# Attention kernel: scores and maxima move into one shared PSUM tile, with one order of steps per head and 17 exponentials of twice the width

## The chip, the cores and the metric

The kernel runs on one core of one Trainium2 chip. The metric is the time of one execution on the device in microseconds (us). Three runs of the kernel before took 2745.0 to 2745.48 us, with a median of 2745.36 us.

## What is computed

Two attention blocks, A and B, read the same `x` of 2048 rows and 512 columns and are mixed by a gate for each row:

```python
def _A_ref(x, wqkv, wo):          # _B_ref is the same with B's weights
    H = 32; Dh = D // H           # 32 heads of 16
    qkv = (x @ wqkv).reshape(B, S, 3, H, Dh).transpose(2, 0, 3, 1, 4)
    q, k, v = qkv[0], qkv[1], qkv[2]
    scores = jnp.einsum("bhqd,bhkd->bhqk", q, k) * (Dh ** -0.5)
    p = _softmax(scores, axis=-1)
    o = jnp.einsum("bhqk,bhkd->bhqd", p, v)
    return o.transpose(0, 2, 1, 3).reshape(B, S, D) @ wo

x = A_x
g = _sigmoid((x * gate_w).sum(-1, keepdims=True))
return g * _A_ref(x, A_wqkv, A_wo) + (1 - g) * _B_ref(x, B_wqkv, B_wo)
```

Two blocks of 32 heads make 64 heads, each with 2048 x 2048 scores of depth 16.

## The kernel before, in words

A first stage projects q, k and v for both blocks and writes them to device memory. Then comes the long stage that the change touches. It counts in rounds, 16 to a head and 1024 in all. A round is 128 keys of one head: four score matmuls (L210), each of 128 keys by 512 queries into one PSUM bank, four exponentials on ScalarE (L212, 512 columns each) that write the tile `p`, and products of `p` with v that TensorE adds up in the bank `acc` (L689). After a head's last round ScalarE copies `acc` out (L710). The row maxima that softmax needs are computed 22 rounds (`NT + LEAD`) ahead, for a later head. For two tiles of 128 queries there are six plain maxima (`max_plain`, a matmul at L148 and a `tensor_reduce` on VectorE at L153) and one pair: `max_rise` puts the positive part of a difference through ScalarE (L160), and `max_pair` lets VectorE add it to a bank of scores and take the maximum (L165).

All matmuls of scores and maxima have 48 or 50 rows, and `rows` (L129) gives them alternately the lower and the upper half of the array, so that two neighbours in TensorE's queue run side by side. The products use the whole array.

PSUM has eight banks of 512 fp32 columns. Before, three of them are the pool `ps_m` (maxima), four the pool `ps_st` (scores and rises), and one is `acc`. Each pool hands out its banks in turn. Each engine works through its own queue in order. What a matmul waits for is the read that last used its bank.

The order of the long stage is written out as strings, one letter for a step: `e` a score and its exponential, `m` a plain maximum, `D` a rise, `A` a pair, and a digit n for n products of a quarter round each (four matmuls of 17 columns and 128 queries for a quarter; neighbouring quarters of one round are joined). `FULL` (L724) covers four rounds, and `EDGE` (L725) replaces halves of it around a head's start and end:

```python
FULL = "mme3emmeem4meeemAe", "3emmeeem3meeemA3DeD"
EDGE = "eemm4mDmemDe3emeemAe", "3emmeeem3emem3eAe"
```

The loop at L744 runs these strings. Where the digit stands, it also starts the projections of finished heads (`project_out`), and one row operation that is due (`row_ops`: gates, reciprocals and a head's `max_split` and `max_rows`). The last 22 rounds, with no maxima left, run `LATE`.

## Time and profile before

| what | value |
|---|---|
| median of 3 runs | 2745.36 us (2745.0 to 2745.48) |
| span of the profiled execution | 2743.5 us; the page has no other time for it |
| granted TensorE clock over the span | 1.000 |
| PE busy | 2733.8 us (100%), 25446 instructions |
| DVE busy | 2411.5 us (88%), 4473 instructions |
| ACT busy | 2410.8 us (88%), 4794 instructions |
| from the first to the last copy of `acc` on ScalarE (62 copies) | 325.0 to 2659.8 us |

A span is the time from the first to the last instruction of one execution as the hardware profiler saw it. Busy time counts an instruction from its start to its end, so an engine whose instructions overlap is counted once. Matmul ends are modelled, and a busy PE can still be waiting. PE is TensorE's matmuls, PEld its weight loads, DVE is VectorE, ACT is ScalarE. "Idle before, released by" in the views names the event that came last before an instruction started.

### The profile page before, as it was taken

To read this page: it belongs to the slowest core of one execution; us is meant where nothing else is said; L and a number is where in the kernel's file an instruction comes from. 1 tells how busy PE (TensorE), PEld (TensorE's weight loads), DVE (VectorE), ACT (ScalarE), POOL (GpSimd) and SP (SyncE) were. 2 spreads that over 40 slices of the span, in tenths; PEclk is the share of its full clock that TensorE was granted. 3 is DMA by queue.
4 is the path that set the end of the run, shared out by engine and by line. 5 is a ranking of instruction groups with operands and counts; after the bars stand their busy time and mean duration, and the time that the engine had idled before them with its cause. 6 is when DMAs were issued, how large, how long until landed. Compare 5 with 4: busy or idle time off the path is not lost.

```text
span 2743.5 us, 64283 instructions
## 1 busy us (share of the span) xinstructions
PE 2733.8 (100%) x25446; PEld 1418.7 (52%) x25446; DVE 2411.5 (88%) x4473; ACT 2410.8 (88%) x4794; POOL 262.2 (10%) x467
## 2 busy tenths in 40 slices
PE   9999999999999999999999999999999999999998
PEld 7787544444444444444444555544444444445543
DVE  5444899999999999999999978899999999998895
ACT  4222899999999999999999978899999999998787
POOL 2010112110000000000100232000000001002202
PEclk9999999999999999999999999999999999999999
DMA  8583434333333233333423534223333333344312
GB/s 286 181 262 153 93 74 81 62 70 62 74 67 60 52 60 67 62 64 62 85 52 54 123 78 92 48 49 62 78 62 63 59 66 65 62 87 83 80 36 95
DMA packets 95603, 231.25 MB, mean 84 GB/s; under 512 B 26182, under 2 KB 35878, under 8 KB 82758
## 3 DMA queue, kind: packets, MB, share of 16 engines
q1 hardware_dynamic: 91590, 216.65, 36.1%
q0 software_dynamic: 2560, 8.91, 1.1%
q8 instruction: 201, 3.29, 0.6%
q10 hardware_dynamic: 1152, 1.57, 0.2%
q14 instruction: 100, 0.82, 0.1%
HBM read 158.13 MB, written 68.94 MB: 83 GB/s over the span
## 4 chain that ended last, share of the span: by engine, by line
PE 99%; DVE 1%; DMA 0%; issue 0%; SPq 0%; DVEq 0%; POOL 0%; POOLq 0%
PE acc L689 38%; PE ps_st L210 24%; PE ps_m L148 19%; PE ps_st L290 6%; PE ps_st L148 5%; PE ps_st L343 3%; PE ps_m L558 3%; PE ps_st L558 0%; PE ps_m L84 0%; PE ps_st L299 0%; DVE o_acc L575 0%; DMA o_num<-od 0%; DVE mxp L153 0%; PE ps_m L210 0%; DVE rise L165 0%; DMA od<-ev 0%
## 5 line engine op out<-in xcount | busy, mean ns | idle before, releaser
L212 ACT ACTIVATE p<-ps_st 128x512 f32<-128x512 f32 x4050 | 2076.8, 629 | 95.3 <-PE ps_m L148 56.1
L153 DVE TENSOR_REDUCE mxp<-ps_m 128x1 f32<-128x512 f32 x3048 | 1934.8, 684 | 125.2 <-PE ps_st L148 46.0
L210 PE MATMUL ps_st<-q_st,k_st 50*128 50x512 f32 x4054 | 1269.5, 433 | 0.0
L148 PE MATMUL ps_m<-k_st,q_st 48*128 48x512 f32 x3548 | 1223.8, 439 | 0.3
L689 PE MATMUL acc<-p,vg 128*17 128x128 f32 (+3 forms) x15664 | 1129.8, 392 | 0.5 <-DVE ev L703 0.4
L210 PEld LDWEIGHTS ps_st<-q_st,k_st 50*128 50x128 f32 x4054 | 614.0, 184 | 436.4 <-ACT p L212 382.7
L148 PEld LDWEIGHTS ps_m<-k_st,q_st 48*128 48x128 f32 x3548 | 604.2, 184 | 268.7 <-DVE mxp L153 222.1
L689 PEld LDWEIGHTS acc<-p,vg 128*17 128x17 f32 x15664 | 323.1, 96 | 404.2 <-issue 330.7
L165 DVE CUSTOM_DVE_ANT_0 rise<-ps_m,rise 128x512 f32<-128x512 f32 x500 | 341.2, 682 | 16.6 <-PE ps_m L148 13.1
L160 ACT ACTIVATE rise<-ps_st 128x512 f32<-128x512 f32 x500 | 300.1, 601 | 16.6 <-PE ps_st L210 0.8
L148 PE MATMUL ps_st<-x_st,q_st 48*128 48x512 f32 x500 | 195.4, 451 | 0.0
L175 POOL CAST mparts<-mrow 128x16 fp32r<-128x16 f32 x64 | 12.7, 198 | 1875.9 <-DVE mrow L174 1875.9
L148 PEld LDWEIGHTS ps_st<-x_st,q_st 48*128 48x128 f32 x500 | 78.0, 184 | 119.5 <-ACT p L212 119.2
L310 ACT CAST part<-ps_st 128x512 fp32r<-128x512 f32 x64 | 37.0, 589 | 111.6 <-PE ps_st L290 95.6
L311 DVE TENSOR_TENSOR part<-ps_st,part 128x512 fp32r<-128x512 f32 x64 | 43.7, 690 | 93.7 <-ACT part L310 70.2
L346 ACT COPY v_st<-ps_st 128x512 f32<-128x512 f32 x32 | 18.8, 588 | 84.2 <-PE ps_st L343 82.5
L558 PE MATMUL ps_m<-wo,ot 128*128 128x512 f32 x348 | 83.0, 393 | 1.0
L558 PEld LDWEIGHTS ps_m<-wo,ot 128*128 128x128 f32 x348 | 64.4, 188 | 19.6 <-issue 4.6
L290 PE MATMUL ps_st<-xh,whi 128*128 128x512 f32 x224 | 59.9, 389 | 0.0
L290 PE MATMUL ps_st<-xh,wlo 128*128 128x512 f32 x224 | 59.9, 389 | 0.0
L290 PE MATMUL ps_st<-xl,whi 128*128 128x512 f32 x224 | 59.9, 389 | 0.0
L545 POOL TENSOR_TENSOR o_num<-o_num,rb 128x512 f32<-128x512 f32 x28 | 35.9, 1287 | 221.7 <-DMA rb<-rd 221.7
(120 smaller groups left out, 946.4 us busy)
## 6 DMA issues: line engine op xcount, KB each, us to landing
k_st<-kd SPq DMA_DIRECT2D x128, 256.0 KB
q_st<-qd SPq DMA_DIRECT2D x128, 256.0 KB
qd<-part SPq DMA_DIRECT2D x32, 512.0 KB
kd<-part SPq DMA_DIRECT2D x32, 512.0 KB
k_st<-kd SPq DMA_DIRECT2D x128, 128.0 KB
q_st<-qd SPq DMA_DIRECT2D x128, 128.0 KB
od<-ev SPq DMA_DIRECT2D x63, 256.0 KB
vd<-v_st SPq DMA_DIRECT2D x32, 272.0 KB
```

The lines of the kernel that those rows point to most:

```text
L148: pe.matmul(ps, q[b:b + SC, t * P:(t + 1) * P], k, start=True, stop=True)
L153: dve.tensor_reduce(o[:, c:c + 1], ps, op=ALU.max, axis=AX.X)
L160: act.activation(rises[m], ps, AF.Relu)
L165: dve.tensor_tensor_reduce(out=rise, in0=ps, in1=rise, scale=1.0, scalar=LOWEST, op0=ALU.add, op1=ALU.max, accum_out=o[:, 0:1])
L210: pe.matmul(ps, k[b:b + SC + 2, kk * P:(kk + 1) * P], q[b:b + SC + 2, cc * 512:(cc + 1) * 512], start=True, stop=True)
L212: act.activation(pt[r][:, c * 512:(c + 1) * 512], ps, AF.Exp, scale=SCALE)
L290: pe.matmul(ps, w[a][:, k], (xh, xl)[b][cc][:, k], start=n == 0, stop=n == 3 * KC - 1)
L310: act.copy(pt[0][:, sl], ps)
L311: dve.tensor_tensor(pt[1][:, sl], ps, pt[0][:, sl].bitcast(F32), op=ALU.subtract)
L343: pe.matmul(ps, a[:, k, o:o + P], b[:, k], start=n == 0, stop=n == 3 * KC - 1)
L558: pe.matmul(ps, ot[a][:, slot, tt * P:(tt + 1) * P], wt[b][:, g], start=first and i == 0, stop=last and i == 2)
L689: pe.matmul(acc[32 * c:32 * c + 17, qa * P:qb * P], v[:, 4 * a + c if final else kt, j], p[:, c * 512 + qa * P:c * 512 + qb * P], start=fi ...
```

## The change

The three PSUM pools become one tile, `ring`, of eight banks. Bank 7 is `acc`. The other seven are handed out by `take`: it keeps a list `age` with the least recently taken bank first, and takes the one at a given rank of that list. Outside the long stage, `m_bank` and `st_bank` restrict this to banks 0 to 2 and 3 to 6. In the long stage of heads 1 to 62 every score, maximum and rise takes its bank from all seven, by the next digit of `RANKS`.

The four-round strings become one string `HEAD` of a head's 16 rounds, run once for each of the heads 1 to 62. Its letters are as before, with three additions: neighbouring `q` are products of a quarter round each, `r` issues `max_split` and then `max_rows`, and `W` is two scores and one exponential over both. A head has 30 `e` and 17 `W` (64 scores), 48 `m`, 8 `A`, 8 `D` and 64 `q` in 20 groups (16 of three and 4 of four). The exponential of a `W` reads its two banks with a stride, so they need not be neighbours: `psb[:, low:high + 1:high - low]`. The first eight rounds of the stage still use `FULL`, and the last 22 `LATE`.

```diff
+NB = 7
...
-    ps_m = ctx.enter_context(tc.tile_pool(name="ps_m", bufs=3, space=PSUM))
-    ps_st = ctx.enter_context(tc.tile_pool(name="ps_st", bufs=4, space=PSUM))
-    ps_acc = ctx.enter_context(tc.tile_pool(name="ps_acc", bufs=1, space=PSUM))
-    acc = ps_acc.tile([P, 512], F32, name="acc")
+    psum = ctx.enter_context(tc.tile_pool(name="psum", bufs=1, space=PSUM))
+    psb = psum.tile([P, NB + 1, 512], F32, name="ring")
+    acc = psb[:, NB]
+    age = list(range(NB))
+
+    def take(rank=0, among=range(NB)):
+        b = [b for b in age if b in among][rank]
+        age.remove(b)
+        age.append(b)
+        return b
+
+    def m_bank():
+        return psb[:, take(0, range(3))]
+
+    def st_bank():
+        return psb[:, take(0, range(3, NB))]
...
+    ranks = []
+
+    def chosen():
+        return psb[:, take(ranks.pop(0))] if ranks else None
...
-        ps = (ps_st if st else ps_m).tile([P, 512], F32, name="ps_st" if st else "ps_m")
+        ps = chosen() or (st_bank if st else m_bank)()
...
     def result_bank():
...
+        return psb[:, take()] if ring else m_bank()
...
+    def score(r, c, n=1):
...
+        chunks = list(range(c, c + n))
+        if n == 2:
+            b0, b1 = take(ranks.pop(0)), take(ranks.pop(0))
+            if b1 < b0:
+                chunks.reverse()
+            wide = [psb[:, b0], psb[:, b1]]
+            ps = psb[:, min(b0, b1):max(b0, b1) + 1:abs(b1 - b0)]
+        elif r < 2 and c % 2:
+            ps = m_bank()
         else:
-            ps = result_bank() if ring else ps_st.tile([P, 512], F32, name="ps_st")
...
+            ps = chosen() or (result_bank() if ring else st_bank())
+        for i, c in enumerate(chunks):
+            kk, cc = (4 * (kt % 4) + c, kt // 4) if h == NH - 1 else (kt, c)
+            b = rows()
+            pe.matmul(wide[i] if n == 2 else ps, k[b:b + SC + 2, kk * P:(kk + 1) * P],
+                      q[b:b + SC + 2, cc * 512:(cc + 1) * 512], start=True, stop=True)
+        c = min(chunks)
+        p = pt[r][:, c * 512:(c + n) * 512]
+        act.activation(p.rearrange("p (n x) -> p n x", n=2) if n == 2 else p, ps, AF.Exp, scale=SCALE)
...
-    FULL = "mme3emmeem4meeemAe", "3emmeeem3meeemA3DeD"
-    EDGE = "eemm4mDmemDe3emeemAe", "3emmeeem3emem3eAe"
+    FULL = "mmeqqqemmeemqqqqmeeemAe", "qqqemmeeemqqqmeeemAqqqDeD"
+    HEAD = ('eqqqrWmmAeqqqWemmDqqqqAemmWqqqWmeAreqqqemmmDeqqqqDmWeAmqqqemWAemqqqemWDmmqqqDmee'
...
+    RANKS = ('01001000200010300000100210200100100110003101000210001031010000100300201000010001'
...
+    def products(n):
+        for a in projects:
+            project_out(*a)
+        projects.clear()
+        turn[0] = 0
+        attend_next(n)
+        if row_ops:
+            fn, *a = row_ops.pop(0)
+            fn(*a)
+
+    def run(order, h=None):
...
+            if step == "q":
+                n = len(order[i:]) - len(order[i:].lstrip("q"))
+                products(n)
+            elif step == "r":
+                steps.pop(0)(h)
+            elif step in "eW":
+                w = 2 if step == "W" else 1
+                score(*next_chunk(w), w)
+            elif step == "m":
+                max_plain(*next(plain))
+            elif step == "D":
+                k = next(to_rise, None)
+                if k is not None:
+                    max_rise(k)
+                elif ranks:
+                    ranks.pop(0)
+            elif step == "A":
+                max_pair(next(pairs))
+            i += n
...
+    for h in range(1, NH - 1):
+        ranks.extend(int(x) for x in RANKS)
+        run(HEAD, h)
```

How the built programs differ is shown at two places, with what each instruction waits for in brackets: `PE_49`, `DVE_49` and `Activation_49` are the counters that TensorE, VectorE and ScalarE raise.

First TensorE's queue in the middle of a head, before. `q_st`, `k_st` and `x_st` are the stacked operands of scores and maxima, L210 a score, L148 a maximum (or, from `x_st`, a rise), L689 products:

```order
L689 MATMUL acc<-p,vg 17x128 x4
L689 MATMUL acc<-p,vg 17x256 x4
L210 MATMUL ps_st<-q_st_160,k_st_161 128x512 [waits Activation_49]
L148 MATMUL ps_m<-k_st_166,q_st_165 128x512 [waits DVE_49] x2
L210 MATMUL ps_st<-q_st_160,k_st_161 128x512 [waits Activation_49] x3
L148 MATMUL ps_m<-k_st_166,q_st_165 128x512 [waits DVE_49]
L689 MATMUL acc<-p,vg 17x256 x4
L689 MATMUL acc<-p,vg 17x128 x4
L148 MATMUL ps_m<-k_st_166,q_st_165 128x512 [waits DVE_49]
L210 MATMUL ps_st<-q_st_160,k_st_161 128x512 [waits Activation_49] x3
L148 MATMUL ps_m<-k_st_166,q_st_165 128x512 [waits DVE_49] x2
L689 MATMUL acc<-p,vg 17x384 x4
```

The same queue near the start of a head, now (L233 a score, L167 a maximum, L714 products):

```order
L233 MATMUL ring<-q_st_158,k_st_159 128x512 [waits Activation_49]
L167 MATMUL ring<-k_st_2139,q_st_2138 128x512 [waits Activation_49]
L233 MATMUL ring<-q_st_158,k_st_159 128x512
L714 MATMUL ring<-p,vg 17x384 x4
L167 MATMUL ring<-k_st_2139,q_st_2138 128x512
L233 MATMUL ring<-q_st_158,k_st_159 128x512 [waits DVE_49] x2
L233 MATMUL ring<-q_st_158,k_st_159 128x512
L167 MATMUL ring<-k_st_2139,q_st_2138 128x512 [waits Activation_49]
L167 MATMUL ring<-k_st_2139,q_st_2138 128x512 [waits DVE_49]
L714 MATMUL ring<-p,vg 17x128 x4
L714 MATMUL ring<-p,vg 17x256 x4
L167 MATMUL ring<-k_st_2139,q_st_2138 128x512
```

Before, a score waits for ScalarE and a maximum for VectorE. Now a bank may have been either's, and two of the maxima here wait for ScalarE. By the ranks, the first two rows write bank 6 and bank 5, and the score ahead of them wrote bank 4: banks 4 and 6 are one `W`. The maximum in bank 5 waits until ScalarE's counter stands at 1215, which is the number that the exponential over banks 4 and 6 itself raises it to. In the eighth row it is the same with bank 4 and the exponential over banks 1 and 6.

Then ScalarE's queue across the end of a head, before (L212 exponentials, L160 rises, L710 the copy of `acc`):

```order
L160 ACTIVATE rise<-ps_st 128x512 [waits DVE_49,PE_49]
L212 ACTIVATE p<-ps_st 128x512 [waits PE_49] x14
L710 COPY ev<-acc 128x512 [waits DMAHW3_49,PE_49]
L212 ACTIVATE p<-ps_st 128x512 [waits PE_49] x4
L160 ACTIVATE rise<-ps_st 128x512 [waits DVE_49,PE_49]
```

And now, from the copy on (L735 the copy, L237 exponentials):

```order
L735 COPY ev<-ring 128x512 [waits DMAHW3_49,PE_49]
L237 ACTIVATE p<-ring 128x1024 [waits PE_49]
L237 ACTIVATE p<-ring 128x512 [waits PE_49] x2
L237 ACTIVATE p<-ring 128x512 [waits PE_49,Activation_49]
L237 ACTIVATE p<-ring 128x1024 [waits DVE_49,PE_49]
L237 ACTIVATE p<-ring 128x512 [waits PE_49]
L237 ACTIVATE p<-ring 128x512 [waits PE_49,Activation_49]
L237 ACTIVATE p<-ring 128x1024 [waits DVE_49,PE_49]
```

Exponentials of 1024 columns stand among those of 512, and some of them wait for VectorE as well as for TensorE. Where one waits for `Activation_49`, it is for an exponential six or more places earlier.

## The prediction

> **What bounds the kernel now.** I read the page's busy times first, then one stretch of the long stage by windows, then the timeline inside it, engine by engine. The copies of `acc` mark the heads, so a source view of L710 gives the length of a head, and a window over the same seven heads gives each engine's work in it (the columns are the window, its length, and the busy time of PE, PEld, DVE, ACT and POOL with counts):

> ```profile
> L710 ACT COPY ev<-acc x8: 589/592/597, 917.5 to 1176.6; 128x512 f32<-128x512 f32 x8
> ...
> 917.50:1176.60 259.10, 259.10 (x2634) 124.72 (x2635) 248.42 (x463) 255.45 (x512) 6.33 (x25) 1.00 0.33 62
> ...
> L710 ACT COPY ev<-acc x62: 587/592/597, 325.0 to 2659.8; 128x512 f32<-128x512 f32 x62
> ```

> Seven heads take 259.1 us, 37.0 us each. ScalarE is busy for 255.45 / 7 = 36.5 us of a head and VectorE for 248.42 / 7 = 35.5 us. Over the whole stage a head takes (2659.8 - 325.0) / 61 = 38.3 us, because some heads share their time with the projections.

> PE's 259.10 of 259.10 says little, since matmul ends are modelled. Its own need comes from the distances between its instructions, in the timeline:

> ```profile
> 1003.36 0.42 PE L148 MATMUL ps_m<-k_st,q_st 48*128 48x512 f32 x1
> 1003.71 1.06 PE L689 MATMUL acc<-p,vg 128*17 128x128 f32 x16
> 1004.70 0.50 PE L148 MATMUL ps_m<-k_st,q_st 48*128 48x512 f32 x1
> ...
> 1009.55 0.84 PE L689 MATMUL acc<-p,vg 128*17 128x384 f32 x8
> ...
> 1010.32 0.50 PE L148 MATMUL ps_st<-x_st,q_st 48*128 48x512 f32 x1
> 1010.32 0.50 PE L210 MATMUL ps_st<-q_st,k_st 50*128 50x512 f32 x1
> ...
> 1010.66 0.40 PE L148 MATMUL ps_st<-x_st,q_st 48*128 48x512 f32 x1
> 1010.67 0.62 PE L148 MATMUL ps_m<-k_st,q_st 48*128 48x512 f32 x2
> ...
> 1010.91 0.41 PE L210 MATMUL ps_st<-q_st,k_st 50*128 50x512 f32 x1
> 1011.25 0.52 PE L689 MATMUL acc<-p,vg 128*17 128x384 f32 x4
> ```

> Score and maximum matmuls start in pairs. After a break the second pair starts 0.34 us after the first (1010.32, 1010.66), later ones 0.23 to 0.25. Products start 0.33 to 0.35 after the last pair, and the next pair follows 0.77 after a product group of three quarters (1009.55, 1010.32) and 0.98 after one of four (1003.71, 1004.70). So a group costs 0.33 + 0.77 = 1.10 or 0.33 + 0.98 = 1.31. A head has 64 pairs in 20 groups and 20 product groups: 20 x 0.34 + 24 x 0.23 + 16 x 1.10 + 4 x 1.31 = 35.2 us. Three engines thus need 36.5, 35.5 and 35.2 us of the 37.0, ScalarE most. That they overlap so well rests on banks: each engine has finished work of TensorE's waiting while it reads.

> **The wide exponentials, by themselves.** ScalarE's spacing of narrow ones, their mean length, and the nearest wide row, a copy from SBUF:

> ```profile
> 921.52 6.01 ACT L212 ACTIVATE p<-ps_st 128x512 f32<-128x512 f32 x12
> 927.63 0.60 ACT L160 ACTIVATE rise<-ps_st 128x512 f32<-128x512 f32 x1
> ...
> L212 ACT ACTIVATE p<-ps_st 128x512 f32<-128x512 f32 x4050 | 2076.8, 629 | 95.3 <-PE ps_m L148 56.1
> ...
> L277 ACT CAST xh<-raw 128x512 fp32r<-128x512 f32 x8 | 4.9, 618 | 1.2 <-DMA raw<-in_xT 1.0
> L277 ACT CAST xh<-vg 128x1024 fp32r<-128x1024 f32 x4 | 4.1, 1054 | 0.0
> ```

> Twelve exponentials take 927.63 - 921.52 = 6.11, 0.51 us each. 512 more columns cost 1054 - 618 = 436 ns, so a wide one holds ScalarE for 0.51 + 0.44 = 0.95 instead of 1.02 and ends 1.05 after its start. 17 x 0.07 = 1.2 us a head comes off ScalarE: 36.5 to 35.3. Bounds are nothing (a wide one costs two) and 17 x (0.629 - 0.436) = 3.3 (all that does not grow with the columns is saved). VectorE keeps its 35.5, TensorE its 35.2, since HEAD has the same matmuls and the same 20 groups as before. If banks let it, the best a head can do is VectorE's 35.5.

> **What the shared tile adds.** The built program orders an access to the tile against everything between its first and its last address. A strided exponential over banks 4 and 6 therefore also counts as a reader of bank 5, and the next writer of 5 waits until it has ended. Counting `take` through RANKS, only 2 of the 17 pairs are neighbours; 7 are two banks apart, 2 three, 3 four and 3 five. Going through one head of the program's waits, 14 matmuls wait for an exponential that never reads their bank, and at least 8 exponentials or maxima wait across ScalarE and VectorE the same way. In ten of the 14 nothing for ScalarE lies between the exponential's second score and the held matmul. In the other four one instruction does.

> The place shown in the change is the plainest: scores in 4 and 6, one exponential over both, and right behind it a maximum in 5. Behind that maximum stands all of TensorE's queue, the next scores for ScalarE and the next maxima for VectorE. Nothing moves until the exponential has ended, and then ScalarE has nothing to do until a new score lands. Two rows price that:

> ```profile
> 1002.63 0.60 ACT L160 ACTIVATE rise<-ps_st 128x512 f32<-128x512 f32 x1
> 1003.28 0.18 PEld L210 LDWEIGHTS ps_st<-q_st,k_st 50*128 50x128 f32 x1 [0.20 <-ACT rise L160]
> ...
> 236.64 0.50 PE L148 MATMUL ps_m<-k_st,q_st 48*128 48x512 f32 x1
> ...
> 237.17 0.69 DVE L153 TENSOR_REDUCE mxp<-ps_m 128x1 f32<-128x512 f32 x1 [1.83 <-PE ps_st L148]
> ```

> ScalarE ends at 1003.23 and the freed weight load starts at 1003.28: 0.05. A matmul that starts at 236.64 is read from 237.17 on: 0.53. From the end of one such exponential to the end of the next, a stretch thus takes at least 0.05, then TensorE's way to the next one's second score, then 0.53 and 1.05: 1.63 plus the way.

> The 14 stretches of a head, with the banks of the exponential that opens each, the matmuls and product groups from the held one to that second score (Q3, Q4: three, four quarters), the way by the distances above, and what ScalarE's or VectorE's queue adds:

> ```
> opened by  matmuls and products        way   queues
> 4,6        2 Q3 4                      1.44  0.4
> 1,6        2 Q3 6                      1.67  1.65
> 1,6        2                           0     0
> 0,5        4 Q3 2                      1.44  0
> 2,4        2 Q4 5                      1.88  0.8
> 0,3        3                           0.34  0
> 4,6        4                           0.34  0.45
> 2,6        3 Q3 4                      1.78  0.15
> 3,6        1 Q3 7 Q3 2                 3.00  0.1
> 1,5        4 Q3 2                      1.44  0
> 0,2        4 Q4 6 Q3 6 Q3 6 Q4 4       7.21  1.6
> 2,4        3 Q3 4                      1.78  0.15
> 0,4        3 Q3 4                      1.78  0.15
> 2,4        2 Q3 6 Q3 7 Q4 5            5.45  0.4
> ```

> The first: a pair, 1.10 for the products, a second pair 0.34 later, the last, 1.44. The ways sum to 29.55, and with 14 x 1.63 = 22.8 that is 52.4 us a head.

> The queues are worked the same way, each instruction starting when its engine is free and its waits are over. VectorE's spacing in the same heads:

> ```profile
> 942.34 3.24 DVE L153 TENSOR_REDUCE mxp<-ps_m 128x1 f32<-128x512 f32 x5
> 945.50 0.68 DVE L165 CUSTOM_DVE_ANT_0 rise<-ps_m,rise 128x512 f32<-128x512 f32 x1
> 946.11 0.08 DVE L165 DVE_READ_ACCUMULATOR2_ANT mxp<- 128x1 f32 x1
> 946.27 1.29 DVE L153 TENSOR_REDUCE mxp<-ps_m 128x1 f32<-128x512 f32 x2
> ```

> A maximum takes (945.50 - 942.34) / 5 = 0.63, a pair 946.27 - 945.50 = 0.77. In the second stretch the exponential over 1 and 6 must wait for the pair in bank 4, which has four maxima ahead of it on VectorE. The first lands 0.05 + 0.53 = 0.58 after the stretch opens, and behind it VectorE never runs dry. At 0.58 + 4 x 0.63 + 0.77 the pair is done, and the exponential starts at 3.9 and not at 1.67 + 0.58 = 2.25: hence 1.65. The long stretch has two such waits, one of them through a group of products that itself waits for ScalarE. All queues together add 5.85, so a head takes 58.2 us, of which ScalarE works 35.3.

> [...]

> **The sum.** Every one of the heads 1 to 62 is changed. 62 x (58.2 - 37.0) = 1314 us more. Added to the median of 2745 that is 4059 us. (The profiled span, 2743.5, is 2 us under the median. The extra work of the projections is taken as it was.) The prologue and the last rounds hand out banks in nearly the same turn as before, and cost nothing that I can see.

> One step is moved: `max_rows`, whose three transfers carry the maxima of a head into its `q` rows, now stands at the second `r`, 11 of a head's 64 scores before the first score that needs them.

> ```profile
> 940.58 0.58 SPq L184 DMA_DIRECT2D md<-mt  x1
> 942.58 0.52 SPq L186 DMA_DIRECT2D q_st<-md  x2
> ```

> The way out takes 2.0 us until the ways back are issued, and they can hardly take longer than that. Eleven scores are 11/64 of 58.2, 10 us. That hides it, even at the old pace (6.4).

> **The rivals.**

> 1. *The queues run beside the waits.* If ScalarE and VectorE catch up within each stretch, only TensorE's way counts: 52.4 a head, 2745 + 62 x 15.4 = 3700 us. For it: I put VectorE's maxima strictly one after another from the moment a stretch opens. Against: the two big entries come from named waits. 0.14.

> 2. *The held matmuls come late anyway: faster.* One mechanism, at the same 14 places: if TensorE reached each held matmul only after the exponential had ended, nothing would be held. Then VectorE's 35.5 sets the pace, and 62 x (37.0 - 35.5) = 93 us go: 2652. It decides from the point where TensorE runs 0.53 + 1.05 = 1.6 us behind the second score. But eight of the 14 held matmuls are the very next one, and the others follow within a group of products (1.1) or two. ScalarE was idle for 3.6 of 259.1 us, so scores were always ready. 0.04.

> 3. *The clock falls.* TensorE would work 35.2 of 58.2 us, 60%. The only stretch of this trace with gaps like that is the end:

> ```profile
> 2720.00:2743.00 23.00, 16.98 (x82) 9.86 (x80) 16.00 (x36) 7.77 (x14) 6.86 (x6) 0.96 0.48 183
> ```

> With PE busy for 16.98 of 23.0 us the granted clock was 0.96. If it went to one half, as an outer case, the ways (29.55) and landings (14 x 0.53) would double: 37 us more a head, 2745 + 62 x (58.2 + 37 - 37.0) = 6350. [...] Here no standstill is over 2 us except where VectorE is waited for, and 0.96 is the lowest window I found. 0.09.

> That the change does not do what it says (wide exponentials no cheaper) moves a head by 1 us and leaves the forecast as it is.

> **How the numbers follow.** The forecast, 58.2 us a head, has 0.72. Its own range is from rival 1's 3700 to the case that a wide exponential takes as long as two narrow ones, 2 x 0.63 = 1.26 and not 1.05: 14 x 0.21 = 2.9 more a head, 2745 + 62 x 24.1 = 4240. I give 3690 to 4250. It leaves out rivals 2 and 3 and 0.01 for no change, 0.14 together. A measurement can tell about 0.2% (5.5 us) from no change. Faster: rival 2, 0.04. Same 0.01. Slower: the rest, 0.95.

> **What would show it.** Right: copies of `acc` some 58 us apart. ScalarE busy for about 60% of the long stage. Its idle time in front of exponentials put down to TensorE, and TensorE's weight loads of scores and maxima waiting more than 1 us for a 1024-wide exponential. ScalarE's work in a head at 35.3. If copies stand 52 us apart, rival 1 holds. A clock under 0.9 in mid-stage shows rival 3. Copies 37 us apart or less, with the 14 matmuls starting without a wait, prove the forecast wrong.

## The result, and the profile after

The changed kernel takes 4786.4 us (median of four runs, 4771.54 to 4823.66), against 2745.3 us before: 1.7455 times as long, 95% interval 1.7421 to 1.749. The forecast of slower holds. The time of 4059 us does not, and the range ended at 4250. The time grew by 2041 us where 1314 were forecast.

The profiled execution after has a span of 4769.5 us. From its page: busy times, the granted clock in 40 slices, and the chain of waits that ended last.

```profile
PE 3857.0 (81%) x24454; PEld 1608.9 (34%) x24454; DVE 2480.9 (52%) x4473; ACT 2503.7 (52%) x3740; POOL 260.4 (5%) x467
...
PEclk9986666666666666666666677778877676777787
...
PE 68%; ACT 19%; DVE 9%; issue 3%; DMA 0%; ACTq 0%; DVEq 0%; POOL 0%; SPq 0%
```

ScalarE and VectorE fell from 88% of the span to 52%. ScalarE now has 19% of the chain. The clock, 1.000 over the whole span before, drops in the third slice and stays between 0.6 and 0.8 through the long stage.

The copies of `acc` mark the heads as before, and two windows of whole heads stand below them (seven heads early in the stage, five late; the last three columns are the clock, the DMA share and GB/s).

```profile
L735 ACT COPY ev<-ring x62: 586/589/605, 341.0 to 4660.0; 128x512 f32<-128x512 f32 x62
...
L735 ACT COPY ev<-ring x8: 586/588/589, 1520.8 to 2035.8; 128x512 f32<-128x512 f32 x8
...
L735 ACT COPY ev<-ring x6: 604/604/605, 3269.5 to 3576.8; 128x512 f32<-128x512 f32 x6
...
1520.80:2035.80 515.00, 409.56 (x2522) 151.82 (x2522) 256.83 (x462) 266.85 (x392) 6.29 (x25) 0.65 0.17 31
3269.50:3576.80 307.30, 236.81 (x1802) 94.56 (x1800) 182.07 (x331) 188.57 (x282) 5.38 (x19) 0.81 0.20 38
```

Where a head took 37.0 us, seven early ones take 515.0 / 7 = 73.6 us at a clock of 0.65, and five late ones 307.3 / 5 = 61.5 us at 0.81. The heads differ because `take` goes on from whatever order the projections left in `age`: from about the 36th head the same ranks give other banks. Counted in the built program, an early head has 14 matmuls that wait for an exponential over banks that they do not touch, a late one 13. The 33 early heads between copies take 73.6 us on average (71.5 to 77.0). The 20 late ones that share no time with projections all have the same order of banks, yet they take from 61.4 us at a clock of 0.81, like the five shown, to 72.0 us at 0.59. Their mean is 64.2.

The view of waits shows who waits for whom now (engine, tile and line, the releaser, us in total, times, longest):

```profile
DVE mxp L172 <- PE ring L167: 1380.2, 914, 3.9
ACT p L237 <- PE ring L233: 963.7, 799, 15.2
PEld ring L167 <- ACT p L237: 911.0, 590, 2.2
...
PEld ring L233 <- ACT p L237: 619.4, 432, 2.5
```

It is the chain of waits that the prediction described: TensorE's weight loads of maxima and scores wait for ScalarE, 911.0 / 590 = 1.5 and 619.4 / 432 = 1.4 us each time, and ScalarE and VectorE then wait for TensorE.

The groups by line show what single instructions cost (columns as in the prediction):

```profile
L237 ACT ACTIVATE p<-ring 128x512 f32<-128x512 f32 x1980 | 1141.0, 603 | 999.6 <-PE ring L233 557.8 <-PE ring L167 437.7
L237 ACT ACTIVATE p<-ring 128x1024 f32<-128x1024 f32 x1054 | 1075.6, 1023 | 631.0 <-PE ring L233 405.9 <-DVE mxp L172 97.7 <-DVE mxp L184 84.5
```

A wide exponential takes 1.02 us, as costed (1.05). The timeline of an early head has the first stretches of the prediction's table, and a surprise in the middle:

```profile
1525.45 0.18 PEld L167 LDWEIGHTS ring<-k_st,q_st 48*128 48x128 f32 x1 [1.63 <-ACT p L237]
...
1529.05 0.29 PEld L167 LDWEIGHTS ring<-k_st,q_st 48*128 48x128 f32 x2 [2.10 <-ACT p L237]
...
1529.78 1.48 PE L714 MATMUL ring<-p,vg 128*17 128x128 f32 x16
...
1531.19 0.79 PE L167 MATMUL ring<-k_st,q_st 48*128 48x512 f32 x1
...
1534.03 1.02 ACT L237 ACTIVATE p<-ring 128x1024 f32<-128x1024 f32 x1 [1.38 <-DVE mxp L184]
1535.11 0.29 PEld L233 LDWEIGHTS ring<-q_st,k_st 50*128 50x128 f32 x2 [1.34 <-ACT p L237]
1535.11 0.80 PE L233 MATMUL ring<-q_st,k_st 50*128 50x512 f32 x2 [0.86 <-ACT p L237]
1535.95 1.02 ACT L237 ACTIVATE p<-ring 128x1024 f32<-128x1024 f32 x1 [0.89 <-PE ring L233]
1537.02 0.50 PEld L167 LDWEIGHTS ring<-k_st,q_st 48*128 48x128 f32 x3 [1.63 <-ACT p L237]
```

The first stretch, from one freed weight load to the next, lasts 1529.05 - 1525.45 = 3.60 us. By the table it is 0.05 + 1.44 + 0.53 + 1.05 + 0.4 = 3.47. A wide exponential ends at 1536.97 and the held load starts 0.05 later, at 1537.02, the 0.05 of the prediction. But after 1529.78 the products take 1531.19 - 1529.78 = 1.41 us to the next pair, where the prediction has 0.77 for their three quarters. The clock by short windows says why:

```profile
1523.80:1528.30 4.50, 2.39 (x17) 0.64 (x15) 2.73 (x6) 3.03 (x5) 0.00 (x0) 1.00 1.12 186
1529.80:1544.80 15.00, 12.30 (x72) 4.29 (x72) 6.36 (x11) 5.35 (x7) 0.00 (x0) 0.50 0.25 35
1546.30:1552.30 6.00, 3.27 (x33) 1.45 (x29) 2.55 (x5) 4.69 (x7) 0.00 (x0) 1.00 0.00 1
1553.80:1570.30 16.50, 13.36 (x69) 5.00 (x70) 7.30 (x14) 7.80 (x12) 0.47 (x3) 0.50 0.01 1
```

The clock is not 0.65. It changes between 1.00 and 0.50. The clock records of this trace hold no other value, and every spell in them but the last lasts a whole multiple of 3.41 us. In these seven heads it is 3.4 to 10.2 us at full clock, mostly 6.8, and 6.8 to 23.9 us at half. 0.65 is the mean. Two causes thus stand to be told apart: the waits for foreign banks, at full clock, and a clock that halves because of the standstills. The theory tested below is that both act, the second because of the first. Its rivals are that the shared tile itself, the new order of steps, or the strided wide exponential is what costs.

### The profile page after: what moved, and what is told of

It reads as the page before. It is cut to its first block, busy times and chain, and to the rows that moved or that the text cites. A ratio compares the mean times of both kernels' runs of the same rounds, so it can differ in the third digit from the quotient of the medians.

```text
span 4769.5 us, 62158 instructions
## 1 busy us (share of the span) xinstructions
PE 3857.0 (81%) x24454; PEld 1608.9 (34%) x24454; DVE 2480.9 (52%) x4473; ACT 2503.7 (52%) x3740; POOL 260.4 (5%) x467
## 4 chain that ended last, share of the span: by engine, by line
PE 68%; ACT 19%; DVE 9%; issue 3%; DMA 0%; ACTq 0%; DVEq 0%; POOL 0%; SPq 0%
PE ring L714 26%; PE ring L167 20%; ACT p L237 19%; PE ring L233 15%; DVE mxp L172 8%; PE ring L315 4%; PE ring L583 2%; PE ring L368 2%; DVE rise L184 1%; ACT rise L179 1%; ACT ev L735 0%; ACTq L237 0%; DMA raw<-in_xT 0%; DMA part<-in_wqkv_a 0%; DVE o_acc L600 0%
## 5 line engine op out<-in xcount | busy, mean ns | idle before, releaser
L237 ACT ACTIVATE p<-ring 128x512 f32<-128x512 f32 (+1 forms) x3034 | 2152.2, 749 | 1630.6 <-PE ring L233 963.7
L172 DVE TENSOR_REDUCE mxp<-ring 128x1 f32<-128x512 f32 x3096 | 2016.1, 687 | 1800.1 <-PE ring L167 1380.2
L167 PE MATMUL ring<-k_st,q_st 48*128 48x512 f32 x3596 | 1516.9, 584 | 542.4 <-ACT p L237 535.9
L233 PE MATMUL ring<-q_st,k_st 50*128 50x512 f32 x4096 | 1530.0, 569 | 311.4 <-ACT p L237 311.4
L714 PE MATMUL ring<-p,vg 128*17 128x256 f32 (+3 forms) x14672 | 1571.3, 544 | 0.5 <-DVE ev L728 0.4
L167 PEld LDWEIGHTS ring<-k_st,q_st 48*128 48x128 f32 x3596 | 651.5, 250 | 1134.7 <-ACT p L237 861.5
L233 PEld LDWEIGHTS ring<-q_st,k_st 50*128 50x128 f32 x4096 | 677.6, 245 | 1047.9 <-ACT p L237 619.4
L714 PEld LDWEIGHTS ring<-p,vg 128*17 128x17 f32 x14672 | 354.2, 112 | 737.3 <-issue 691.4
L179 ACT ACTIVATE rise<-ring 128x512 f32<-128x512 f32 x500 | 299.7, 600 | 384.8 <-PE ring L167 382.2
L184 DVE CUSTOM_DVE_ANT_0 rise<-ring,rise 128x512 f32<-128x512 f32 x500 | 342.9, 686 | 275.8 <-PE ring L167 165.7
L167 PE MATMUL ring<-x_st,q_st 48*128 48x512 f32 x500 | 292.5, 610 | 37.8 <-ACT p L237 37.8
L167 PEld LDWEIGHTS ring<-x_st,q_st 48*128 48x128 f32 x500 | 122.4, 260 | 133.1 <-ACT rise L179 52.7
L335 ACT CAST part<-ring 128x512 fp32r<-128x512 f32 x64 | 37.1, 589 | 111.7 <-PE ring L315 90.4
L735 ACT COPY ev<-ring 128x512 f32<-128x512 f32 x62 | 36.7, 592 | 29.9 <-PE ring L714 29.8
```

Source lines behind the costliest of these rows:

```text
L167: pe.matmul(ps, q[b:b + SC, t * P:(t + 1) * P], k, start=True, stop=True)
L172: dve.tensor_reduce(o[:, c:c + 1], ps, op=ALU.max, axis=AX.X)
L179: act.activation(rises[m], ps, AF.Relu)
L184: dve.tensor_tensor_reduce(out=rise, in0=ps, in1=rise, scale=1.0, scalar=LOWEST, op0=ALU.add, op1=ALU.max, accum_out=o[:, 0:1])
L233: pe.matmul(wide[i] if n == 2 else ps, k[b:b + SC + 2, kk * P:(kk + 1) * P], q[b:b + SC + 2, cc * 512:(cc + 1) * 512], start=True, stop=True)
L237: act.activation(p.rearrange("p (n x) -> p n x", n=2) if n == 2 else p, ps, AF.Exp, scale=SCALE)
```

## The experiments

**One tile, and nothing else (before's order).** The three pools become slices of one eight-bank tile, the order of steps stays.

```diff
-    ps_m = ctx.enter_context(tc.tile_pool(name="ps_m", bufs=3, space=PSUM))
...
+    psb = psum.tile([P, 8, 512], F32, name="ring")
...
+    ps_m, ps_st = Banks(0, 3), Banks(3, 4)
```

> The kernel before with its order, and its three pools replaced by eight banks of one tile, taken in the same turn. Held-matmul theory: no strided read, no change, 2740 to 2750 us. Rival, one tile for all banks adds waits by itself: above 2800 us.

Measured: 2745.09 us, ratio 1.0001 (0.9992 to 1.0011). The shared tile by itself costs nothing that can be measured.

**Every wide exponential split in two.** Tile, order and ranks of the changed kernel, but no access covers more than its own bank.

```diff
...
-        act.activation(p.rearrange("p (n x) -> p n x", n=2) if n == 2 else p, ps, AF.Exp, scale=SCALE)
+        for i, c in enumerate(chunks):
+            act.activation(pt[r][:, c * 512:(c + 1) * 512], wide[i] if n == 2 else ps, AF.Exp, scale=SCALE)
```

> The changed kernel with its order, ranks and shared tile, but each wide exponential split into two narrow ones over the same two banks, so that no read spans a bank between. Held-matmul theory: nothing is held, heads go back to 35.5 to 38.5 us, 2650 to 2840 us in all, clock 1.0. Rival, the new order or the seven shared banks are what breaks the overlap: heads stay above 50 us, over 3500 us. Rival, the wide exponentials as instructions are slow: 2650 to 2840 too, not told apart here.

Measured: 2765.9 us, ratio 1.0075 (1.0059 to 1.009). Its copies of `acc`, seven ordinary heads and the four heads that share their time with the first projections:

```profile
L734 ACT COPY ev<-ring x8: 667/674/677, 917.7 to 1177.1; 128x512 f32<-128x512 f32 x8
...
L734 ACT COPY ev<-ring x5: 665/673/678, 1547.5 to 1751.1; 128x512 f32<-128x512 f32 x5
```

An ordinary head takes (1177.1 - 917.7) / 7 = 37.1 us, as before. The new order and the moved `max_rows` cost it nothing. The four heads take 203.6 us, where the trace of before has 193.3 for them:

```profile
L710 ACT COPY ev<-acc x5: 589/591/597, 1547.0 to 1740.3; 128x512 f32<-128x512 f32 x5
```

These and the last four heads make up the 20 us. The granted clock over this window is 0.97, so part of the 10 us may be the clock's. All but 20 of the 2041 us therefore hang on the exponentials being wide.

**17 wide exponentials a head, over neighbouring banks only.** As many and as wide as in the change, but nothing lies between their banks.

```diff
-            b0, b1 = take(ranks.pop(0)), take(ranks.pop(0))
+            del ranks[:2]
+            near = min(range(NB - 1), key=lambda b: max(age.index(b), age.index(b + 1)))
+            b0, b1 = [take(0, (near, near + 1)) for _ in range(2)]
```

> The changed kernel, but the two banks of a wide exponential are always neighbours (the least recently used neighbouring pair), still 17 wide ones a head. Held-matmul theory: no bank lies between, so nothing is held for a foreign bank; ranks no longer fit, so 2680 to 2950 us, clock 1.0. Rival, wide exponentials as such are slow or hold TensorE through two banks at once: above 3500 us.

Measured: 2787.64 us, ratio 1.0156 (1.0141 to 1.0171). Seven heads and the window over them:

```profile
L737 ACT COPY ev<-ring x8: 607/607/612, 929.4 to 1193.9; 128x512 f32<-128x512 f32 x8
...
917.00:1182.00 265.00, 263.70 (x2532) 120.73 (x2536) 249.68 (x468) 253.92 (x394) 6.31 (x25) 1.00 0.33 61
```

A head takes 264.5 / 7 = 37.8 us at full clock. So it is not the width that costs 2041 us, but what lies between the banks of a wide access. Nor is it the stride as such: a wide exponential takes 1031 ns here and 1023 ns in the changed kernel. The width is no gain either, though. To that the last three experiments return.

**One strided wide exponential a head.** The split kernel, with the ninth `W` of each head wide again: banks 4 and 6, a maximum in bank 5 right behind it.

```diff
+        if n == 2 and (nth[0] - 1) % 17 in (8,):
...
+            act.activation(p.rearrange("p (n x) -> p n x", n=2), ps, AF.Exp, scale=SCALE)
```

> The kernel with all wide exponentials split in two, except for one a head: banks 4 and 6, with the maximum in bank 5 right behind it. One matmul a head is held. If a hold costs its share of the 14, (58.2 - 37) / 14 = 1.5 us: 62 x 1.5 = 93 us over the split kernel's 2766, 2859. If a single hold is swallowed by the finished work that waits in the banks: 2766 to 2775. Clock 0.98 or more in both.

Measured: 2889.68 us, ratio 1.0518 (1.048 to 1.0556), 31 us above the 2859 of the expectation. Three windows, one of four heads at full clock and two of a single head each:

```profile
827.78:981.51 153.73, 148.91 (x1442) 72.55 (x1442) 141.98 (x269) 146.56 (x289) 1.89 (x12) 1.00 0.32 56
...
402.30:442.11 39.81, 38.61 (x362) 18.58 (x362) 35.58 (x67) 36.70 (x74) 8.52 (x16) 0.96 0.43 88
1136.52:1177.83 41.31, 40.10 (x362) 19.19 (x362) 35.56 (x67) 36.69 (x73) 0.47 (x3) 0.92 0.30 52
```

At full clock a head takes 153.73 / 4 = 38.4 us: 1.4 us for one held matmul, where the prediction's per-stretch working makes it 21.2 / 14 = 1.5. Most ordinary heads are like that. But eight of them take 39.8 us and three take 41.3, with the same instructions and a lower clock. In the head of 41.3 us the clock goes like this:

```profile
1120.00:1136.50 16.50, 16.50 (x171) 8.52 (x171) 15.73 (x33) 16.27 (x33) 0.47 (x3) 1.00 0.02 5
1138.52:1140.52 2.00, 0.89 (x7) 0.42 (x5) 1.74 (x4) 2.00 (x4) 0.00 (x0) 1.00 1.02 269
1140.52:1142.52 2.00, 1.90 (x14) 0.93 (x16) 0.69 (x1) 0.65 (x2) 0.00 (x0) 0.85 1.14 166
1142.52:1148.52 6.00, 6.00 (x48) 2.67 (x46) 3.88 (x7) 3.26 (x6) 0.00 (x0) 0.50 1.02 148
1148.52:1150.52 2.00, 2.00 (x20) 0.78 (x16) 1.55 (x3) 1.71 (x4) 0.00 (x0) 0.95 0.58 50
1150.52:1177.80 27.28, 27.28 (x272) 13.59 (x270) 25.76 (x50) 27.04 (x55) 0.47 (x3) 1.00 0.01 4
```

The standstill near 1140 (0.89 busy of 2.00) in the timeline:

```profile
1140.62 0.50 PE L167 MATMUL ring<-k_st,q_st 48*128 48x512 f32 x1 [1.21 <-ACT p L241]
```

TensorE stands still for 1.2 us, and within 2 us its clock halves. It gets back to 1.00 only near 1148.6 although TensorE has no pause any more: 0.15 x 2 / 0.5 + 6.00 + 0.05 x 2 / 0.5 = 6.8 us at half. In the head at 402 the spell lasts 3.41 us by the clock records. This is the clock's price without any change of the work: 1.4 and 2.9 us.

**Nine of the 17 wide.** The changed kernel, with the last eight `W` of a head split: 6 held matmuls in an early head, 5 in a late one.

```diff
+        if n == 2 and (nth[0] - 1) % 17 in range(9):
...
+            act.activation(p.rearrange("p (n x) -> p n x", n=2), ps, AF.Exp, scale=SCALE)
```

> The same with nine of the 17 wide exponentials a head kept, the first nine of the string, which hold six matmuls a head in the first half of the heads and five in most others. At 1.5 us a hold: 62 x 5.6 x 1.5 = 520 us over 2766, 3290, at full clock. If the clock falls with the standstill in proportion (0.65 at 14 holds): about 0.85 and 3500 us. If it falls only past some share of standstill: 0.97 or more and about 3290.

Measured: 3635.64 us, ratio 1.3213 (1.3167 to 1.3258), above all three figures of its expectation. Two early heads and one late one:

```profile
1088.02:1197.19 109.17, 92.96 (x722) 39.05 (x722) 73.05 (x136) 74.53 (x129) 0.94 (x6) 0.81 0.24 40
...
2352.00:2395.94 43.94, 38.10 (x362) 17.25 (x364) 35.57 (x67) 36.74 (x64) 0.47 (x3) 1.00 0.28 48
```

The late head, at full clock, takes 43.9 us: 6.9 / 5 = 1.4 us for each held matmul again. So holds add up. Other late heads with the same order of banks take up to 51.8 us, at 0.80. The early heads shown take 54.6 us at 0.81, while 37.0 + 6 x 1.4 = 45.4 would be their length by the holds alone. The other 9 us go with the clock.

**Zero matmuls in the standstills.** The changed kernel with all 17 wide, and ahead of each held matmul a few matmuls of zeros that are added to `acc`: 6 where the held one is next in the queue, 1 where products stand between, 70 in an early head and 58 in a late one. They change no result and remove no wait. They only keep TensorE busy: for 184.27 of 194.56 us in the early heads below, where it was 409.56 of 515.00 without them.

```diff
...
+        for _ in range(1 if since[0] else 6):
+            pe.matmul(acc, none[:48], ident[:48].unsqueeze(1).to_broadcast([48, 4, P]), start=False, stop=False,
...
```

> The changed kernel with some 70 matmuls of zeros a head added in front of the held matmuls (they add 0 to the accumulator bank, six before a matmul that comes at once, one where products stand between), so that TensorE works while it stands still. If the clock is a second cause: granted clock above 0.95, heads 56 to 62 us, 3950 to 4300 us, although more matmuls run. If the lower clock is only a sign of the standstill and costs nothing: 4770 us or more.

Measured: 4340.0 us, ratio 1.5789 (1.5752 to 1.5825). More work on TensorE made the kernel 446 us faster. The time is 40 us above the first range of the expectation, and the clock over the whole profiled run is 0.89, not 0.95. Windows over three early and five late heads:

```profile
1392.52:1587.08 194.56, 184.27 (x1292) 74.32 (x1294) 109.02 (x199) 113.64 (x169) 3.64 (x12) 0.87 0.20 37
2912.44:3184.99 272.55, 254.09 (x2092) 105.68 (x2090) 181.10 (x335) 187.30 (x282) 5.39 (x19) 1.00 0.24 44
```

The late heads shown run at 1.00, and a head takes 272.55 / 5 = 54.5 us, where the same 13 holds without the zeros cost 61.5 at 0.81. Not all late heads do: others with the same banks take up to 68.9 us at 0.73. The early heads got from 0.65 to 0.87 and take 64.9. At full clock the second stretch of a late head can be held against the prediction's working (opened by banks 1 and 6, 3.9 us from its start to the exponential that ends it):

```profile
2976.01 0.50 PE L181 MATMUL ring<-k_st,q_st 48*128 48x512 f32 x2 [0.15 <-ACT p L252]
...
2976.55 2.50 DVE L186 TENSOR_REDUCE mxp<-ring 128x1 f32<-128x512 f32 x4 [1.50 <-PE ring L181]
...
2978.96 0.68 DVE L198 CUSTOM_DVE_ANT_0 rise<-ring,rise 128x512 f32<-128x512 f32 x1
...
2979.77 1.02 ACT L252 ACTIVATE p<-ring 128x1024 f32<-128x1024 f32 x1 [1.38 <-DVE mxp L198]
```

The exponential before it ended at 2975.96, the first maximum starts 0.59 later (0.58 forecast), four of them and the pair follow without a gap, and the wide exponential starts at 3.81. VectorE's strict queue, on which rival 1 turned, is as the prediction had it.

**Another list of zeros.** A list of its own for the places of an early head, 83 a head. Against the rule of the first version it differs at five of the 15 places that the rule finds in an early head: 10, 6 and 6 stand where there was 1, and 5 and 1 where there were 6.

```diff
...
+    FILL = 6, 6, 10, 6, 6, 5, 1, 6, 6, 6, 6, 1, 6, 6, 6
...
+        for _ in range(FILL[(place[0] - 1) % 15]):
```

> As the run with matmuls of zeros in front of held matmuls, with more of them at the two places where TensorE stands longest because VectorE is waited for (ten and five there). In the first half of the heads the clock should come from 0.87 to 0.95 or more, and a head from 65 us to 57 to 60, the prediction's 58.2 without a loss of clock: 3900 to 4200 us in all. If the clock is not what makes the difference: 4340 or more, since there are more matmuls.

Measured: 4615.61 us, ratio 1.6843 (1.6764 to 1.6921), a miss in total: it lies where the expectation put a clock that makes no difference. The heads say otherwise. Its windows over five early and five late heads:

```profile
465.08:772.83 307.75, 284.96 (x2217) 118.52 (x2219) 181.26 (x331) 189.59 (x281) 35.47 (x69) 1.00 0.24 47
3495.35:3853.76 358.41, 340.19 (x2157) 143.27 (x2155) 182.28 (x335) 188.72 (x282) 11.02 (x25) 0.76 0.19 36
```

The early heads shown now run at 1.00, at 307.75 / 5 = 61.5 us instead of 73.6. 21 of the 33 early ones are like them (61.5 to 61.8 us), and the others take up to 80.3 us at 0.70. In the late heads, whose holds stand elsewhere, the list doesn't fit, and they take 71.7 us at 0.76. Between them the two kernels give both kinds of head at full clock: 61.5 us with 14 holds, 54.5 with 13.

**Does a wide exponential pay at all, without holds?** Before's order with 14 wide exponentials a head over neighbouring score banks, wherever two scores stand side by side:

```diff
+        return r >= 2 and not ring and c < 3 and order.startswith("ee") and ps_st.next % 4 < 3
...
+        act.activation(pt[r][:, c * 512:(c + 2) * 512].rearrange("p (n x) -> p n x", n=2), psb[:, b0:b0 + 2],
...
```

> The order before with its string and its turn of banks in one tile, and 14 wide exponentials a head over two neighbouring banks of the four score banks, wherever two scores of a round follow each other there. Nothing is held for a foreign bank. Wide exponentials as such save 14 x 0.07 to 0.1 us of ScalarE a head: 2745 - 62 x 1.0 to 1.4 = 2660 to 2685 if banks allow. Rival: two banks freed at once instead of one after the other cost as much: 2735 to 2800.

Measured: 2821.72 us, ratio 1.0278 (1.0261 to 1.0295), above both ranges of the expectation. ScalarE's work fell and the head got longer (copies and window of seven heads):

```profile
L735 ACT COPY ev<-ring x8: 585/586/587, 939.0 to 1207.1; 128x512 f32<-128x512 f32 x8
...
938.98:1207.12 268.14, 268.14 (x2634) 121.39 (x2636) 249.80 (x463) 251.44 (x414) 6.30 (x25) 1.00 0.33 60
```

ScalarE's busy time is 251.44 us for seven heads instead of 255.45, a saving of 4.01 / 98 = 0.04 us for each wide one. A head takes 38.3 us. From 940 to 1200 us the wide exponentials wait 7.5 us for the matmuls of their own scores (19 times) and other scores' weight loads 16.5 us for a wide one (47 times), where in the trace of before the exponentials wait 0.2 us for a matmul in the same window. That this comes from the first bank, which two narrow exponentials would free one exponential earlier, is an estimate from what the wide form changes. No run isolates it.

**Only four of them,** where the pair stands alone in front of a maximum (`order.startswith("eem")`, the step before no `e`).

> The order of before in one tile; only four exponentials a head are 1024 wide, each over two neighbouring score banks that come free together and are not wanted at once. If a wide exponential saves its 0.07 to 0.1 us wherever nobody waits for the two banks, a head gets 0.3 to 0.4 us shorter and the time is 2720 to 2735 us. If the late freeing of the first of two banks is paid here too, as in the kernel with 14 of them, the time is 2745 to 2765 us.

Measured: 2745.46 us, ratio 1.0001 (0.9992 to 1.001). The very bottom of the second expectation: no gain, and no loss that can be measured.

```profile
918.11:1177.28 259.17, 259.17 (x2634) 123.51 (x2636) 248.34 (x463) 253.79 (x485) 6.30 (x25) 1.00 0.33 62
```

ScalarE is busy for 253.79 us instead of 255.45, and seven heads take 259.2 us as before. So a small relief of ScalarE did not shorten the 37.0.

**The changed order, wide only where it is cheap.** Two versions without foreign holds: a neighbouring pair among the three longest idle banks, else two narrow ones; and the given ranks, wide only where the two given banks are neighbours.

```diff
...
+            if max(age.index(near), age.index(near + 1)) < 3:
...
+        if n == 2 and abs(b1 - b0) == 1:
...
```

> The changed order, with an exponential 1024 wide only where two neighbouring banks are among the three that have been idle longest, 9 to 17 a head, the others split in two; no matmul is held for a foreign bank. If the loss of 0.7 us a head in the kernel with 17 neighbouring pairs came from taking banks too early, the time lies between 2690 and 2766 us, at or below that of the split kernel. If reading two banks at once costs by itself, it lies between 2766 and 2800 us.

> The changed order with the banks as given; an exponential is 1024 wide only where the two banks given happen to be neighbours, 2 to 4 a head, the others split in two; no matmul is held for a foreign bank. If those few save 0.07 to 0.1 us each, the time is 2745 to 2760 us, below the 2766 of the split kernel; if reading two banks at once costs more than it saves, it is 2766 us or more.

Measured: 2779.0 us (ratio 1.0124, 1.0109 to 1.014) with 9 to 17 wide a head, and 2761.84 us (1.0059, 1.0046 to 1.0071) with 2 to 4. Against 2765.9 with none and 2787.64 with 17, few wide ones gain 4 us in all, many lose 13 to 22. The gain is not the wide ones' own as far as can be seen: in the profiled runs the 53 ordinary heads differ by 1 us, and the other 4 lie in the heads that share their time with projections, where the split kernel's clock has five half spells of 3.4 us and this one's three. The first version is in the costly half of its expectation, the second just above its gain of 2745 to 2760. No version that was run beats the kernel before.

## Why the prediction was right and wrong

**Right: the mechanism, and nearly its price at full clock.** The extra time comes from matmuls held for an exponential that never reads their bank. Splitting the exponentials takes it away, neighbouring banks take away all but 0.8 us a head, one strided exponential brings back 1.4 us. With the clock held at 1.00 by zeros, an early head takes 61.5 us and a late one 54.5. The 33 early heads would add 33 x (61.5 - 37.0) = 809 us and the 20 late ones that share no time with projections 20 x (54.5 - 37.0) = 350, together 1159. The prediction's 21.2 us a head make 1124 for these 53. That close a match is partly luck. It took one head for all 62, and came near the mean of two kinds that lie 7 us apart. And how much of the 61.5 is the zeros' own time is open: 14 x 1.4 on top of 37.0 would be 56.6.

**Wrong: rival 3, the clock.** It got 0.09, and was priced only as an outer case of half clock throughout. The step that failed is "Here no standstill is over 2 us except where VectorE is waited for, and 0.96 is the lowest window I found". Both halves misled. With one strided exponential a head, a standstill of 1.2 us was followed by 6.8 us at half, and with 14 held matmuls a head the clock is at half for 70% of the time ((1 - 0.65) / 0.5). And the 0.96 was a mean that had to be split:

```profile
2720.00:2740.50 20.50, 16.98 (x82) 9.86 (x80) 16.00 (x36) 7.77 (x14) 6.86 (x6) 1.00 0.48 183
2741.00:2743.00 2.00, 0.00 (x0) 0.00 (x0) 0.00 (x0) 0.00 (x0) 0.00 (x0) 0.50 0.34 131
```

In the trace of before the clock is 1.00 while TensorE works, and 0.50 from 3.5 us after its last matmul, which ends at 2737.45. The row said nothing of a mild loss of 4%. It showed the clock at 0.50 after the work had stopped. In the changed kernel, whose weight loads wait 1.4 to 1.5 us on average for ScalarE, standstills were enough: the clock swings between 1.00 and 0.50, with a mean of 0.65 in the early heads, while it is 1.00 in the ordinary heads of the split version, which has no holds. The prediction set the clock aside as if standstills of up to 2 us were harmless, and no row of before shows that.

What the clock took: 33 x (73.6 - 61.5) = 399 us in the early heads, and 1283 - 20 x 54.5 = 193 in the 20 late ones, which take 1283 us together. That makes 592 of the 2041 us, beside the 1159. Eight heads share their time with projections. They grew by 234 us, and no run shows how much of that is the clock. The other 56 us lie before the first copy of `acc`, after the last one, and between the profiled run and the median. The late heads show the clock's price without any zeros too: the same instructions and banks take 61.4 us at 0.81 and 72.0 us at 0.59.

The mixed price could not be had from the trace of before, which does not show how long the clock stays at half. With the 70% of the run, TensorE's mean speed is 0.65, and the ways (29.55) and landings (7.4) of the prediction grow by 37 x (1 / 0.65 - 1) = 20 us. The measured growth of an early head is 12 over the 61.5 with zeros and 15 over the 58.2. Why it is less than 20 is open.

**Right in the parts:** the 0.05 from the end of an exponential to the freed load, 0.05 measured. A wide exponential, 1.05 against 1.02. The first stretch, 3.47 against 3.60 at full clock. The second, 3.9 against 3.81. Rival 1 falls with it. Rival 2 falls by 590 + 432 waits of 1.5 us. `max_rows` costs an ordinary head nothing.

**Wrong without effect on the sum:** "17 x 0.07 = 1.2 us a head comes off ScalarE". Where the wide ones run without holds, 0.04 us each comes off at 14 a head, and nothing of it reaches the time. In the changed kernel ScalarE's busy time is 266.85 / 7 = 38.1 us a head and not 35.3, because narrow exponentials that wait for their score overlap less: 1980 of them are 1141.0 us of busy time, 0.58 each, where the 4050 of before are 2076.8, 0.51 each. What sets 37.0 us in the kernel before is not settled. ScalarE alone hardly does (four wide ones relieve it by 0.2 us a head for nothing), and TensorE's 35.2 may be counted too low.

## What to carry to other kernels

Before an access is made wider or strided, ask what the program's order will take it to cover: here all that lay between its ends belonged to it, and the next writer there waited (TensorE for 1.2 us at the one strided exponential of a head, a head 1.4 us longer). Whoever prices new standstills of TensorE must price the clock with them, as a mixture of full and half and not as an outer case, take the share of half from a run that has such standstills (70% with 14 holds a head here), and read a mean clock only after cutting its window into its states. Where one unit's order depends on a state that others change (here `age`), price the second kind of unit too.

## What the runs showed that was not expected

- Clock against standstills, in ordinary heads: no hold 1.00, one hold a head 1.00 with spells at half in 11 heads, five 0.80 to 1.00 in the late heads of the version with nine wide ones, six 0.74 to 0.86 in its early heads, thirteen 0.59 to 0.81, fourteen 0.59 to 0.69. These are means. The clock records hold 1.00 and 0.50 and nothing in between, and the spells are whole multiples of 3.41 us, but for the one that follows the last matmul of a run.
- Zero matmuls were enough to hold the clock: with 58 in a late head it goes from 0.81 to 1.00, with 83 in an early one from 0.65 to 1.00, and a head gets 7 or 12 us shorter, if they stand at the right places. Even then not every head is held. At wrong places the late heads went to 71.7 us, all 16 of the last ones, where without zeros they take 61.4 to 72.0.
- The copy of `acc` takes 674 ns in the split kernel and 589 to 591 before and after the change, at the same shape. Why is open.
